# PSUM banks and ScalarE copies in a fused attention and SwiGLU kernel: three banks for attention, two for down-projection groups, the first term of p by ScalarE while groups run, and every third down weight split three beats sooner

## The chip, the cores and the metric

The kernel runs on one core of one Trainium2 chip. The core has a matrix engine (TensorE, PE in the profile; its weight loads are the row PEld), VectorE (DVE), ScalarE (ACT), GpSimd (POOL) and SyncE (SP), which only issues DMAs here. Each engine takes its own instructions in the order in which they stand in its program; waits between engines go by semaphores. Matmul results go to PSUM, which this kernel uses as eight banks of 128 x 512 float32. The metric is the device time of one execution in microseconds; a comparison uses the median of several.

## The reference

One layer's input x (2048 x 576) goes through two branches, mixed by a sigmoid gate. Branch A is attention with 32 heads of 18 in four segments of 512 rows, each segment softmaxed causally within itself and adding a linear memory of the segments before. Branch B is a SwiGLU feed-forward with 4608 hidden units.

```python
g = _sigmoid((x * gate_w).sum(-1, keepdims=True))
a = _A_ref(x, A_wq, A_wk, A_wv, A_wo, A_beta)
b = _B_ref(x, B_w_gate, B_w_up, B_w_down)
return g * a + (1 - g) * b
...
logits = jnp.einsum("bhqd,bhkd->bhqk", qs, ks) * scale + mask
p = _softmax(logits, axis=-1)
a_dot = jnp.einsum("bhqk,bhkd->bhqd", p, vs)
...
return (_silu(x @ w_gate) * (x @ w_up)) @ w_down
```

Everything is float32. The kernel keeps that precision by splitting operands into a high and a low part and adding the products high x high, high x low and low x high.

## The kernel before, in words

The program is one long stream, written out by hand (the schedule is manual, so instructions stand in the order in which Python emits them). It has three stages: projections, memory updates and the gate; the main loop, in which the feed-forward and the attention run interleaved; and the output projection.

**The main loop** goes over `seq`: two halves of the rows (1024 each), and within each half 36 blocks `f` of 128 hidden units. One block makes gate and up for 128 units and 1024 rows with seven products instead of eight (a Strassen-like scheme). Each product, `seven`, is six matmuls of L985 and one of L988. ScalarE and VectorE evict and combine the results in three banks of their own (a, x, y: banks 0, 1, 2), at L1042 to L1067, and the hidden units are then split into `hh` (high, on ScalarE) and `hl` (low, on VectorE).

After each product comes a `tick`, eight per block, counted k = 0 to 7. A tick first issues loads of the down weight (`draw`, 128 x 576) and its split, where the tables say so, then calls `beat`. A beat does three things, in this order:
1. It runs the functions that are due. `defer(k, fn)` puts a function k beats ahead. Weight preparation hangs on this: sums on GpSimd (L245), high parts on ScalarE (L249), low parts on VectorE (L252), and the residue rows of the weights (`r_block`), which are stored in three parts: the high part `rt` (L231) is stored twice (L228), then VectorE overwrites `rt` with the low part (L232), which is stored too. L232 has to wait until the first stores have read `rt`. `BLOCKS` says which blocks of the first half make residues: 3, 6, 9, ..., 30, two each in the first four of them.
2. It runs down-projection groups, as many as `SHARE[k]` says: 0, 0, 2, 2, 3, 3, 3, 3. A group (`down_group`) is nine matmuls (L844) for 128 rows and 320 or 256 output columns over three blocks f, and its sum is added to `ya` on VectorE (L849, the first time a copy, L847).
3. Between the groups it advances the attention generator by one step, as far as its credit reaches.

Every third block (f % 3 == 0, f > 0) starts by queueing 16 groups, and its eight beats work them all off; such a block is called a group block here. While groups are queued a beat is busy and gives attention one step per odd-numbered slot; in the two blocks between, it gives about three steps per block. At the change of halves, ten beats without products (`BREAK`) work off the last 16 groups of the first half, while the operands of the second half (`xo`) are split.

**One attention step** (`att_gen`, tau) handles three score tiles at different stages. `p_bank(tau - 3)` makes p's first term (L745, float32 to float16) and, on GpSimd, its second (L746: what the first leaves over). `e_bank(tau - 1)` makes the exponentials (L731, ScalarE) and masks the diagonal on GpSimd (L739). `s_bank(tau)` makes scores (L713, TensorE) and their row bound `mb` (L719, VectorE), which the exponentials need. `x_bank(tau - 5)` transposes p by DMA (`pt`, L750, issued by SyncE), and every sixth step `v_unit` multiplies five transposed tiles with the values (L761, L762) and VectorE reduces the result (L768). Score tiles and value tiles take turns on the banks of `ts_tile`. A matmul that starts a new tile in a bank has to wait until the engine that reads the old one is done: L731 for a score tile, L768 for a value tile, L849 for a down group. p and the exponentials have four buffers each, transposed p has seven.

**Down weights**: `d_load` at ticks (0, 3), (1, 3), (2, 2), given as (f % 3, k); `d_split` at ticks (1, 1), (1, 7), (2, 7) queues the high part on ScalarE for that beat (L927), the low part on VectorE for the next (L928) and, in the fifth, a store of both to DRAM (`dc`, L826), from where the second half fetches them.

Of the kernel before, what the change touches and what calls it, by code (L numbers as in the profile page):

```python
# [16 lines left out]
AF = mybir.ActivationFunctionType  # L17
# [3 lines left out]
P = 128  # L21
# [44 lines left out]
def gated_mix(ctx, tc, xT, xrest, wf, wfr, wfh, wd, wv, wo, beta, cmask, ident, bmask, out):  # L66
    nc = tc.nc
# [31 lines left out]
    def banks(*ids):  # L99
        turn = cycle(ids)  # L100
        return lambda shape=(P, L): ps.tile(list(shape), F32, name=f"bank{next(turn)}")
# [3 lines left out]
    pair_tile = banks(3, 4)  # L105
# [4 lines left out]
    a_tile = banks(0)  # L110
    x_tile = banks(1)
    y_tile = banks(2)
    ts_tile = banks(5, 6)
    group_tile = banks(3, 4, 7)

    def split(hi, lo, src):
        nc.scalar.activation(hi, src, AF.Copy)  # L117
# [87 lines left out]
    def d_load(f):  # L205
        r = fp.tile([P, D], F32, name="draw", bufs=1)
        nc.sync.dma_start(r, wd[f])
        return r
# [468 lines left out]
    with ExitStack() as st:  # L677
        cps = []
# [63 lines left out]
        def p_bank(z):  # L742
            pe = cur.pop(("e", z))
            p = cur["p", z] = ap.tile([P, 2, L], F16, name="p", bufs=4)
            nc.vector.tensor_copy(p[:, 0], pe)  # L745
            nc.gpsimd.tensor_sub(p[:, 1], pe, p[:, 0])  # L746

        def x_bank(z):
# [36 lines left out]
        def att_gen():  # L785
# [5 lines left out]
            for tau in range(N + 10):  # L791
                u, n = divmod(tau, 6)
                if n == 2 and sends:
                    nc.sync.dma_start(*sends.pop(0))
                if 1 <= n <= 3 and u + 1 < 2 * NB:
                    for d in stack_loads(u + 1)[3 * n - 3:3 * n]:
                        nc.sync.dma_start(*d)
                if n == 2 and u > 1 and u % 2 == 1 and (u - 3) // 2 < NB:
                    o_step((u - 3) // 2)
                z = at(tau - PL)  # L800
                if z is not None:
                    p_bank(z)
                z = at(tau - 1)
                if z is not None:
                    e_bank(z)
                z = at(tau)
                if z is not None:
                    s_bank(z)
                if n == 5 and 1 <= u <= 2 * NB:
                    v_unit(u - 1)  # L810
                    if u % 4 == 1 and u // 4 + 1 < 4 * NSEG:
                        v_fetch(u // 4 + 1)
                z = at(tau - XL)
                if z is not None:
                    x_bank(z)
                yield
# [6 lines left out]
        def d_split(f, r):  # L823
            d = d_tile()
            split_by(1, d[:, 0], d[:, 1], r)
            defer(5, lambda: nc.sync.dma_start(dc[f], f32(d).rearrange("p a n -> p (a n)")))  # L826
            return d

        def d_fetch(f):
            d = d_tile()  # L830
            nc.sync.dma_start(f32(d).rearrange("p a n -> p (a n)"), dc[f])
            return d

        def down_group(c, i, hf, hs, ws, ya, half):
            b, k = divmod(i, 4)
            cs = (slice(0, 320), slice(320, D))[hf]
            t = (pair_tile if cps else group_tile)([P, 320])[:, :cs.stop - cs.start]
            n = 0
            for f in range(CH * c, CH * c + CH):
                hh, hl = (z[:, b, P * k:P * k + P] for z in hs[half, f])  # L840
                d = ws[half, f]
                dh, dl = d[:, 0], d[:, 1]
                for p, q in ((hh, dh), (hh, dl), (hl, dh)):
                    nc.tensor.matmul(t, p, q[:, cs], start=(n == 0), stop=(n == 3 * CH - 1))  # L844
                    n += 1
            if c == 0:
                nc.vector.tensor_copy(ya[:, i, cs], t)  # L847
            else:
                nc.vector.tensor_add(ya[:, i, cs], t, ya[:, i, cs])  # L849
            if c == FT // CH - 1 and hf and half == 0:  # L850
                stores.append((ffd[i], ya[:, i]))
# [5 lines left out]
        def c_open():  # L857
            if cps:
                return
            ast.close()  # L860
            cps.append(pool(st, "cp", 2, side="right"))
            for hf in range(2):
                wos.append(cps[0].tile([P, 2, NT, 288], F32R, name=f"wo{hf}", bufs=1))
            for n, (hf, z) in zip((1, 2, 4, 5, 8, 9), ((0, 0), (0, 1), (0, 2), (1, 0), (1, 1), (1, 2))):
                wo_load(n, hf, slice(96 * z, 96 * z + 96))
            defer(2, lambda: tiles.update({0: c_load(0)}))
            defer(6, lambda: tiles.update({1: c_load(1)}))
# [53 lines left out]
        defer(6, lambda: v_fetch(0))  # L921
        groups = []
        credit = [-1.0]
        yas = {}

        def split_by(k, hi, lo, src):
# [3 lines left out]
        def beat(k=None, half=0):  # L930
            for fn in due.popleft() if due else ():
                fn()
            busy = 1 if groups else 0
            share = 2 if k is None else SHARE[k]
            for n in range(max(share, 1)):
                if groups and n < share:
                    down_group(*groups.pop(0))
                if n % 2 or (not busy and (n or k in QUIET)):
                    continue
                credit[0] += 0.5 if k is None else TICK[half][busy]  # L940
                if credit[0] >= 1:
                    credit[0] -= 1
                    if next(att, att) is att:
                        c_open()
# [48 lines left out]
        for pos, (half, f) in enumerate(seq):  # L993
            if f == 0:
                yas[half] = yp.tile([P, 8, D], F32, name="ya")
            q = f % CH
# [21 lines left out]
            def tick():  # L1018
                k = step[0]
                step[0] += 1  # L1020
                if k == 0:
                    while stores:
                        nc.sync.dma_start(*stores.pop(0))
                if half == 0:
                    if (q, k) in ((0, 3), (1, 3), (2, 2)):
                        draw[f] = d_load(f)
                    if (q, k) in ((1, 1), (1, 7), (2, 7)):
                        g = f - 1 if k == 1 else f
                        ds[half, g] = d_split(g, draw.pop(g))
                elif (q, k) in ((1, 0), (1, 2), (2, 1)):  # L1030
                    g = f - 1 if k == 0 else f
                    ds[half, g] = d_fetch(g)
                beat(k, half)
# [7 lines left out]
            seven(a, 0)  # L1041
            nc.scalar.activation(xx, a, AF.Copy)  # L1042
            tick()
            seven(y, 1)
            nc.scalar.activation(p5, y, AF.Copy)
# [29 lines left out]
            if f == FT - 1:  # L1075
                groups += feed(half, f)
                if half == 0:
                    for n in range(BREAK):
                        beat(None if n > 1 else n)
                    XO, XR = X2, XR2  # L1080
                    assert not groups
# [13 lines left out]
        def downs(k):  # L1095
            for _ in range(min(k, len(groups))):
                down_group(*groups.pop(0))

        ffs = {n: f_load(n) for n in range(2)}
        for n in range(17):  # L1100
# [6 lines left out]
            if n:  # L1107
                tt = order[n - 1]
                ff = ffs.pop(n - 1)
                for hf in range(2):  # L1110
                    c = slice(288 * hf, 288 * hf + 288)
                    t = chain_tile()
# [67 lines left out]
```

## Time and profile before

| | us |
|---|---|
| median of 3 runs (1762.95 to 1763.73) | 1763.63 |
| the profiled execution | 1765.94 |
| its span, first to last instruction | 1764.2 |
| TensorE busy in the span | 1720.6 |
| clock granted to TensorE, mean | 0.993 |

Rows are read like this. In the busy table and the windows, a number is busy time in us, with the count of instructions in brackets; a window's row ends with the granted clock, the mean share of DMA engines that were busy, and GB/s. In the waits, `PE bank L713 <- ACT pe L731: 13.2, 19, 1.2` says that the TensorE instruction of line 713 that writes a bank waited for the ScalarE instruction of line 731 that writes pe: 13.2 us in all, 19 times, 1.2 us the longest. A group of instructions has line, engine, operation, out<-in, shapes and count, then busy us and mean ns of one, then the idle time before them and who ended it. In the timeline a row starts with its start in us from the span's start and its duration in us; square brackets hold the idle time of that engine just before it and what ended it. Two instructions of an engine may overlap slightly. Buffer numbers are left out of names.

### The profile page before, as it was taken

The numbers are of one execution on the slowest core, as the hardware profiler recorded it, in microseconds if no ns is written. First come the engines' busy times: TensorE is split into PE (matmuls) and PEld (weight loads), VectorE is DVE, ScalarE is ACT, GpSimd is POOL, SyncE is SP. The second block draws the span as 40 slices with busy tenths as digits, with TensorE's granted clock in tenths as the row PEclk, the third lists the DMA queues.
The fourth block names the chain that finished last, engine by engine and source line by source line (L and its number), as shares of the span: only waits on it lengthen the run. The fifth ranks groups of instructions, "written<-read, shape, count | busy, mean of one in ns | idle before, by whom it ended". The sixth has DMA issues, their size and how long they took to land.

```text
span 1764.2 us, 34937 instructions
## 1 busy us (share of the span) xinstructions
PE 1720.6 (98%) x11868; PEld 1490.4 (84%) x11868; DVE 1366.7 (77%) x3239; ACT 1095.4 (62%) x2201; POOL 933.7 (53%) x1194
## 2 busy tenths in 40 slices
PE   9999999999999999999998999999999999999999
PEld 7898978788888888887887888888888888888899
DVE  6566578888898888888888677788788777887655
ACT  7665575775676577566656756665766576556511
POOL 4434545566565655655556455555555555555221
PEclk9999999999999999999999999999999999999999
DMA  8653489898998988898979976876777677756534
GB/s 283 222 188 117 164 287 192 209 223 178 220 221 197 186 190 205 174 203 186 202 163 250 280 163 137 187 169 160 160 175 169 150 165 180 169 129 150 166 129 141
DMA packets 524003, 328.06 MB, mean 186 GB/s; under 512 B 411184, under 2 KB 460336, under 8 KB 523824
## 3 DMA queue, kind: packets, MB, share of 16 engines
q1 hardware_dynamic: 523824, 325.83, 75.3%
q8 instruction: 93, 1.52, 0.4%
q14 instruction: 86, 0.70, 0.1%
HBM read 165.76 MB, written 76.09 MB: 137 GB/s over the span
## 4 chain that ended last, share of the span: by engine, by line
PE 76%; ACT 11%; DVE 4%; DMA 3%; issue 3%; POOL 2%; SPq 1%; DVEq 0%; ACTq 0%; POOLq 0%
PE bank L985 27%; PE bank L844 25%; PE bank L140 10%; PE bank L988 4%; PE bank L713 3%; PE bank L761 2%; ACT L1059 2%; ACT pe L731 1%; ACT L978 1%; PE bank L762 1%; PE bank L399 1%; ACT row L1059 1%; DMA pt<-p 1%; ACT bank L1042 1%; PE bank L445 1%
## 5 line engine op out<-in xcount | busy, mean ns | idle before, releaser
L746 POOL TENSOR_TENSOR p<-pe,p 128x512 f16<-128x512 f32 x320 | 374.3, 1170 | 474.7 <-DVE p L745 447.6
L844 PE MATMUL bank<-dw,hh 128*128 128x320 f32 (+1 forms) x2304 | 492.4, 306 | 3.0 <-ACT hh L117 2.9
L844 PEld LDWEIGHTS bank<-dw,hh 128*128 128x128 f32 x2304 | 384.4, 191 | 14.1 <-ACT hh L117 3.1
L731 ACT ACTIVATE pe<-bank,mb 128x512 f32<-128x512 f32 (+3 forms) x512 | 246.1, 522 | 227.3 <-DVE mb L719 224.5
L844 PE MATMUL bank<-dw,hl 128*128 128x320 f32 (+1 forms) x1152 | 342.1, 297 | 0.0
L719 DVE CUSTOM_DVE_ANT_0 scr<-bank,cm 128x512 bf16<-128x512 f32 (+3 forms) x512 | 246.1, 481 | 7.3 <-PE bank L713 0.6
L849 DVE TENSOR_TENSOR ya<-bank,ya 128x320 f32<-128x320 f32 x352 | 158.1, 453 | 82.8 <-PE bank L844 81.9
L844 PEld LDWEIGHTS bank<-dw,hl 128*128 128x128 f32 x1152 | 219.5, 191 | 0.2 <-DVE hl L118 0.2
L988 PE MATMUL bank<-xr,rh 128*128 128x512 f32 x504 | 196.6, 390 | 0.0
L739 POOL TENSOR_SCALAR_AFFINE_SELECT pe<-pe 128x256 f32<-128x256 f32 (+1 forms) x320 | 150.2, 470 | 31.4 <-ACT pe L731 25.9
L745 DVE CAST p<-pe 128x512 f16<-128x512 f32 x320 | 144.3, 451 | 1.4 <-DMA pt<-p 1.4
L713 PE MATMUL bank<-kst,qst 108*128 108x512 bf16 (+3 forms) x512 | 125.2, 306 | 13.3 <-ACT pe L731 13.2
L245 POOL TENSOR_TENSOR ws<-raw 128x256 f32<-128x256 f32 x140 | 120.9, 864 | 18.3 <-DVE wo__22862 L252 4.1
L988 PEld LDWEIGHTS bank<-xr,rh 128*128 128x128 f32 x504 | 94.7, 188 | 20.5
L928 DVE TENSOR_TENSOR hl<-row,hh 128x512 fp32r<-128x512 f32 x120 | 100.9, 841 | 10.7 <-ACT hh L927 10.3
L1052 ACT ACTIVATE row<-bank 128x512 f32<-128x512 f32 x72 | 43.1, 599 | 100.3 <-PE bank L988 100.2
L1057 DVE TENSOR_TENSOR row<-bank,row 128x512 f32<-128x512 f32 x72 | 49.6, 689 | 59.0 <-ACT bank L1056 58.8
L1059 ACT ACT_TABLE_LOAD x72 | 92.4, 1283 | 1.3
L978 ACT ACT_TABLE_LOAD x72 | 92.4, 1283 | 1.0
L761 PE MATMUL bank<-v,pt 128*128 128x57 bf16 x1280 | 77.6, 188 | 12.0 <-ACT pe L731 10.9
L713 PEld LDWEIGHTS <-qst 108*128 108x128 bf16 x512 | 35.8, 98 | 63.1 <-issue 47.0
L140 PE MATMUL bank<-xo,qhi 128*128 128x512 f32 x264 | 83.1, 396 | 0.0
(2165 smaller groups left out, 4114.0 us busy)
## 6 DMA issues: line engine op xcount, KB each, us to landing
raw<-in_wf_dram SPq DMA_DIRECT2D x140, 256.0 KB
rh<-rc SPq DMA_DIRECT2D x72, 336.0 KB
dc<-dw SPq DMA_DIRECT2D x36, 576.0 KB
dw<-dc SPq DMA_DIRECT2D x36, 576.0 KB
stk<-q SPq DMA_DIRECT2D x32, 384.0 KB
draw<-in_wd_dram SPq DMA_DIRECT2D x36, 288.0 KB
rc<-rt SPq DMA_DIRECT2D x42, 224.0 KB
vd<-vps SPq DMA_DIRECT2D x8, 912.0 KB
```

What stands on the lines that cost most here:

```text
L140: nc.tensor.matmul(t, st[n], mv[n], start=(n == 0), stop=(n == 13))
L713: nc.tensor.matmul(t[:, c:c + w], qs[:KR, pr, P * i:P * i + P], ks[:KR, pr, 0:w], start=True, stop=True)
L719: nc.vector.tensor_tensor_reduce(scr[:, :w], t[:, c:c + w], cm[:, L - w:L], -SCALE, 3.0e38, OP.add, OP.min, m[:, k:k + 1])
L731: nc.scalar.activation(pe[:, c:c + w], t[:, c:c + w], AF.Exp, bias=m[:, k:k + 1], scale=SCALE)
L739: nc.gpsimd.affine_select(d, d, pattern=pat, compare_op=OP.is_ge, fill=0.0, base=0, channel_multiplier=1)
L745: nc.vector.tensor_copy(p[:, 0], pe)
L746: nc.gpsimd.tensor_sub(p[:, 1], pe, p[:, 0])
L844: nc.tensor.matmul(t, p, q[:, cs], start=(n == 0), stop=(n == 3 * CH - 1))
L849: nc.vector.tensor_add(ya[:, i, cs], t, ya[:, i, cs])
L985: nc.tensor.matmul(t, w[:, p, z], x[z][:, q], start=first and n == 0, stop=False, skip_group_check=True)
L988: nc.tensor.matmul(t, rem[:, RPOS[j]], XR[j], start=False, stop=True, skip_group_check=True)
L1059: nc.scalar.activation(sg0, sg0, AF.Silu)
```

## The change

`ts_tile` takes turns on banks 5, 6, 7 instead of 5, 6. `group_tile` (banks 3, 4, 7) goes; down groups always use `pair_tile` (banks 3, 4). p's first term is a ScalarE activation (Copy) in beats that begin with groups queued, and stays on VectorE in the others. The third split of down weights is queued at tick (2, 4) instead of (2, 7).

```diff
-    ts_tile = banks(5, 6)
-    group_tile = banks(3, 4, 7)
+    ts_tile = banks(5, 6, 7)
...
             p = cur["p", z] = ap.tile([P, 2, L], F16, name="p", bufs=4)
-            nc.vector.tensor_copy(p[:, 0], pe)
+            if mode[0]:
+                nc.scalar.activation(p[:, 0], pe, AF.Copy)
+            else:
+                nc.vector.tensor_copy(p[:, 0], pe)
             nc.gpsimd.tensor_sub(p[:, 1], pe, p[:, 0])
...
-            t = (pair_tile if cps else group_tile)([P, 320])[:, :cs.stop - cs.start]
+            t = pair_tile([P, 320])[:, :cs.stop - cs.start]
...
         credit = [-1.0]
+        mode = [0]
...
-            busy = 1 if groups else 0
+            busy = mode[0] = 1 if groups else 0
...
-                    if (q, k) in ((1, 1), (1, 7), (2, 7)):
+                    if (q, k) in ((1, 1), (1, 7), (2, 4)):
```

In the built program the order on TensorE and GpSimd is the same as before but for bank names; 219 instructions go from VectorE to ScalarE; and twelve splits of down weights, with their stores in SyncE's queue, stand earlier.

## The prediction

> **What bounds the kernel now.** I read the page's totals, then the windows of the main loop on TensorE alone, then TensorE's waits.
>
> ```profile
> PE 1720.6 (98%) x11868; PEld 1490.4 (84%) x11868; DVE 1366.7 (77%) x3239; ACT 1095.4 (62%) x2201; POOL 933.7 (53%) x1194
> ...
> 300.00:940.00 640.00, 625.05 (x4493) 1.00 0.87 196
> 1000.00:1620.00 620.00, 614.18 (x4389) 1.00 0.73 164
> ...
> PE bank L713 <- ACT pe L731: 13.2, 19, 1.2
> PE bank L761 <- ACT pe L731: 10.9, 8, 4.1
> PE bank L761 <- DMA pt<-p: 1.0, 3, 0.5
> ```
>
> TensorE is busy for all but 43.6 us of 1764.2, so this change can only win idle time, not work. In 300 to 940 us it idles 14.95 us, in 1000 to 1620 us 5.82 us, and nearly all of that has one name: a score matmul (L713) or the first value matmul (L761) waits until the exponentials (L731) have read the bank that it wants to overwrite. That is 13.2 + 10.9 = 24.1 us in 27 waits. The same waits, asked for by stretch:
>
> ```profile
> PE bank L713 <- ACT pe L731: 9.6, 13, 1.2
> PE bank L761 <- ACT pe L731: 4.6, 5, 1.8
> ...
> PE bank L713 <- ACT pe L731: 3.6, 6, 0.9
> PE bank L761 <- ACT pe L731: 2.2, 2, 1.2
> ```
>
> The first pair is 260 to 945 us (14.2 us, 18 waits), the second 1000 to 1660 us (5.8 us, 8 waits); the remaining one, the longest of the whole run at 4.1 us, is at the change of halves. The exponentials are late because of VectorE, which hands out work strictly in order:
>
> ```profile
> POOL p L746 <- DVE p L745: 447.6, 277, 5.5
> ACT pe L731 <- DVE mb L719: 224.5, 127, 4.6
> ...
> L745 DVE CAST p<-pe 128x512 f16<-128x512 f32 x320 | 144.3, 451 | 1.4 <-DMA pt<-p 1.4
> L354 ACT ACTIVATE q<-qr 128x512 bf16<-128x512 f32 x36 | 22.5, 624 | 7.5 <-DVE qr L351 6.9
> L927 ACT ACTIVATE dw<-draw 128x576 fp32r<-128x576 f32 x36 | 24.2, 673 | 0.0
> L928 DVE TENSOR_TENSOR dw<-draw,dw 128x576 fp32r<-128x576 f32 x36 | 28.6, 796 | 4.5 <-ACT dw L927 4.5
> ```
>
> ScalarE idles 224.5 us waiting for the row minimum (L719), GpSimd 447.6 us for the first term of p (L745); both stand in VectorE's queue.
>
> **The third attention bank.** Score and value tiles take turns on three banks instead of two, so a tile waits for the reader of the tile three back. All 27 waits end on the tile two back; the tile three back was read at least 1.7 us, mostly 5 to 9 us, before the stalled matmul could have started (the readers' ends against the matmuls' starts, tile by tile). So all 24.1 us of this wait go; the question is what is late next. I split them.
> (a) Eleven of the 18 waits before 945 us fall on the first ticks of a block with down groups, 8.5 us in all, and all 8 after 1000 us, 5.8 us: ScalarE and VectorE recover there, since the groups give them time. I count 14.3 us as won.
> (b) Seven, from the first to the last row below, fall in the block just before, where every tick is a 1.6 us gate product and both helper engines are full: 5.7 us.
>
> ```profile
> 324.69 0.19 PE L761 MATMUL bank<-v,pt 128*128 128x57 bf16 x1 [1.00 <-ACT pe L731]
> 814.39 0.38 PE L713 MATMUL bank<-kst,qst 108*128 108x128 bf16 x2 [1.17 <-ACT pe L731]
> 816.61 0.70 DVE L1049 TENSOR_TENSOR bank<-bank,row 128x512 f32<-128x512 f32 x1
> 817.95 0.53 PE L985 MATMUL bank<-xo,wo__11068 128*128 128x512 f32 x1
> 940.49 0.38 PE L713 MATMUL bank<-kst,qst 108*128 108x128 bf16 x2 [1.15 <-ACT pe L731]
> ```
>
> At 814 us, with the 1.17 us gone, the product at 817.95 would come at 816.8, but it overwrites the bank that L1049 reads until 817.3: 0.5 us of 1.17 are lost again. I take half of 5.7: 2.9 us (from 0 to all of it).
>
> **p's first term on ScalarE.** While groups are queued, 219 of the 320 copies move (the instruction order of the changed kernel). VectorE loses 219 x 0.451 = 99 us. A ScalarE cast from SBUF to f16 is not in the trace; the bf16 one of the same shape takes 0.624 us, so ScalarE gets 137 us more and goes from 62% to 70%. It has cover: the 224.5 us of waiting for minima, which also shrink because two copies leave the queue ahead of them. Behind a copy on ScalarE stand the exponentials and the products' evictions, and behind those TensorE; without cover a copy costs up to 0.62 us there. The eviction that TensorE needs first in these blocks (L1042) is issued before the copy, so I take 0. The copy also takes over the wait for the transpose that still reads p's old buffer: 1.4 us over 320 so far, taken as 0 more, up to 1.7 us each where it is late (the rc<-rt wait below). Earlier p should shorten the 1.0 us for transposes; I take half, 0.5 us.
>
> **Two banks for down groups.** A group lasts about 1.2 to 1.6 us and its sum (L849) frees the bank; now it must be done when the group after next starts. In the trace it would be late 49 times. Two kinds:
>
> ```profile
> 460.68 0.42 DVE L745 CAST p<-pe 128x512 f16<-128x512 f32 x1
> 462.54 0.95 DVE L745 CAST p<-pe 128x512 f16<-128x512 f32 x1
> 465.65 0.48 DVE L849 TENSOR_TENSOR ya<-bank,ya 128x320 f32<-128x320 f32 x1
> ...
> 465.37 0.30 PE L844 MATMUL bank<-dw,hh 128*128 128x320 f32 x1
> ...
> 468.51 0.54 SPq L228 DMA_DIRECT2D rc<-rt  x1
> 472.85 0.62 DVE L232 TENSOR_TENSOR rt<-rr,rt 128x448 fp32r<-128x448 f32 x1 [1.68 <-DMA rc<-rt]
> 473.39 0.48 DVE L849 TENSOR_TENSOR ya<-bank,ya 128x320 f32<-128x320 f32 x1
> 472.23 0.31 PE L844 MATMUL bank<-dw,hh 128*128 128x320 f32 x1
> ```
>
> First group: its sum ends at 466.13, the third group starts at 465.37, 0.76 us late. But 0.42 + 0.95 us of copies ahead of it go, and so does the down weight's 0.8 us: no wait. Fifth group: VectorE stands 1.68 us before L232 for a store, and the sum ends at 473.87, 1.64 us after the seventh group's start at 472.23. No copy lies between, so this remains, shortened only by as much as GpSimd, which waits for copies less, makes rt's input earlier; I take 0.8 us in the early blocks that still make such residues and 0.2 us in the later ones. The worst lateness of each group block, summed, is 9.1 us; I take 4.5 us (from 1 to 9).
>
> **Every third weight split three beats sooner.** Twelve times 0.67 us on ScalarE and 0.80 us on VectorE leave the crowded first beats of a group block for the fifth and sixth beat before it: same sum. ScalarE could stand there for the load:
>
> ```profile
> 632.14 0.59 SPq L207 DMA_DIRECT2D draw<-in_wd_dram  x1
> 635.25 0.60 ACT L1056 ACTIVATE bank<-bank 128x512 f32<-128x512 f32 x1
> 464.31 0.42 SPq L826 DMA_DIRECT2D dc<-dw  x1
> ```
>
> The tightest case leaves 3.7 us from issue to the end of L1056, after which the split now stands; the other eleven leave more. The store rc<-rt above took 4.3 us from issue to release, so 0 to about 0.6 us; I take 0. Behind the split stand SiLU's table and SiLU, needed by nothing for 1 us. The store dc<-dw moves three beats up SyncE's queue, past loads and two transposes, at 0.42 us of issue each: off the path, 0 (up to 1 us if a transpose is pushed into a value tile).
>
> **The change of halves.**
>
> ```profile
> 951.92 0.21 PE L761 MATMUL bank<-v,pt 128*128 128x57 bf16 x1 [4.09 <-ACT pe L731]
> 957.66 0.31 PE L844 MATMUL bank<-dw,hh 128*128 128x320 f32 x1
> ...
> 953.78 0.84 ACT L731 ACTIVATE pe<-bank,mb 128x256 f32<-128x256 f32 x2 [1.39 <-DVE mb L719]
> 954.51 0.63 ACT L117 ACTIVATE xo<-wo__12969 128x512 fp32r<-128x512 f32 x1
> ...
> 955.17 1.30 DVE L118 TENSOR_TENSOR xo<-wo__12969,xo 128x512 fp32r<-128x512 f32 x1 [0.22 <-ACT xo L117]
> 956.39 1.65 DVE L928 TENSOR_TENSOR hl<-row,hh 128x512 fp32r<-128x512 f32 x1
> 957.96 0.81 DVE L849 TENSOR_TENSOR ya<-bank,ya 128x320 f32<-128x320 f32 x2
> ...
> 951.90:957.20 5.30, 5.28 (x55) 5.28 (x55) 5.04 (x10) 2.88 (x6) 4.24 (x4) 0.50 1.09 363
> ```
>
> The 4.09 us wait goes, and the first two groups run early. The third group then needs the first one's bank, and that sum stands behind two splits for the second half, which stand behind two exponentials on ScalarE. With two p copies ahead of them there, ScalarE ends the xo split about where it does now, the sum ends near 958.1 instead of 958.43, and the third group starts there instead of 957.66. TensorE also runs at 0.50 of its clock until 957.20 after its wait; a new wait of some 5 us would bring that back for the 3 to 5 us behind 958.1, half of which is about 2.2 us. So nothing of 4.1 us is won and 2.6 us are lost (from a win of 1 to a loss of 5).
> [...]
>
> **The sum.** Won 14.3 + 2.9 + 0.5 = 17.7 us; lost 4.5 + 2.6 = 7.1 us; net 10.6 us. The profiled execution took 1765.94 us (its span 1764.2), so it would take 1755.3; the median of the runs is 2.3 us lower, 1763.63 - 10.6 = 1753.0 us.
>
> **Rivals.**
> - All of it is won: copies leave VectorE and the sums are never late. 14.3 + 5.7 + 1.0, and at the change of halves 2: 23 us, 1741. For: ScalarE's and GpSimd's idle times; against: L232 waits for a store, not for a copy.
> - The next wait takes its place: (b) returns whole, half of (a) too as ScalarE, with 137 us more, is late with evictions, and sums cost 7: 17.7 - 2.9 - 7 - 7 - 2.6 leaves about -1.8, 1765: no change beyond noise. For: both helpers are full in the blocks between; against: ScalarE waits over 1 us before most exponentials.
> [...]
> [...]
>
> **How the numbers follow.** Forecast 62%, all won 13%, no change 13%, slower 12%. The forecast's own range is 5 to 17 us of gain, 1747 to 1759. For 8 in 10: the low end takes (b) whole, 1 us of late sums, and nothing at the change of halves, 20 us, 1743; the high end half of (b), half of (a) lost and 7 us of late sums, hardly a gain, 1763. What a measurement of this kernel can tell is 0.2%, 3.5 us: faster 62 + 13 + 5 of the no-change cases = 80%; same 9%; slower 11%.
>
> **What would show it.** L713 and L761 waiting for L731: near 0. A new row L844 waiting for L849: 3 to 8 us, its longest at the change of halves, near 955. L745 on ScalarE near 0.62 us, 219 of them; ScalarE's waits for minima well under 224 us, GpSimd's waits for p too. L985 waiting for L1049 or L1042: 2 to 4 us. Wrong if L844's waits exceed 15 us, if between 300 and 1620 us a clock of 0.50 shows anywhere but at the change of halves, or if evictions on ScalarE stall TensorE in group blocks.

## The result, and the profile after

The changed kernel takes 1767.69 us (median of 17 runs, 1765.04 to 1772.16) against 1763.35 us for the kernel before (17 runs, 1761.57 to 1765.73). The ratio is 1.0026, 95% interval 1.0019 to 1.0034: 0.26% or 4.3 us slower, where 10.6 us faster was forecast and 1743 to 1763 us was the range.

The profiled execution of the changed kernel took 1767.69 us, its span 1766.0 us. The profiled execution of before was 2.6 us above its own median, so this pair of profiles differs by less than the medians do. First the busy totals and three groups of instructions of the changed kernel, then TensorE's waits. Lines have moved: L844 is now L846 (down groups), L849 is L851 (their sums), L713 is L712, L761 is L763, L731 is L730, L719 is L718, L232 is L231, L252 is L251; p's first term is L745 on ScalarE and L747 on VectorE.

```profile
PE 1723.4 (98%) x11868; PEld 1485.0 (84%) x11868; DVE 1280.7 (73%) x3020; ACT 1208.3 (68%) x2420; POOL 932.3 (53%) x1194
...
L748 POOL TENSOR_TENSOR p<-pe,p 128x512 f16<-128x512 f32 x320 | 381.0, 1193 | 391.5 <-DVE p L747 182.8
L846 PE MATMUL bank<-dw,hh 128*128 128x320 f32 (+1 forms) x2304 | 495.8, 308 | 21.6 <-DVE ya L851 17.0
L846 PEld LDWEIGHTS bank<-dw,hh 128*128 128x128 f32 x2304 | 382.0, 190 | 40.9 <-DVE ya L851 25.7
...
L730 ACT ACTIVATE pe<-bank,mb 128x512 f32<-128x512 f32 (+3 forms) x512 | 246.6, 522 | 119.1 <-DVE mb L718 118.9
...
L745 ACT ACTIVATE p<-pe 128x512 f16<-128x512 f32 x219 | 135.8, 625 | 14.1 <-DMA pt<-p 8.3
```

```profile
PE bank L846 <- DVE ya L851: 17.0, 21, 3.0
...
PE bank L763 <- DMA pt<-p: 2.9, 2, 1.6
...
PE bank L846 <- DVE ya L849: 1.8, 2, 1.3
PE bank L988 <- DVE bank L1052: 1.6, 2, 1.1
```

The load moved, though by less than forecast: 86 us left VectorE (99 forecast), 113 us came to ScalarE (137 forecast). ScalarE's waits for minima shrank from 224.5 to 118.9 us. GpSimd's waits for p's first term were 447.6 us, all for VectorE; now they are 182.8 us for VectorE and, where the term comes from ScalarE, 156.5 us for ScalarE:

```profile
POOL p L748 <- DVE p L747: 182.8, 94, 5.3
POOL p L748 <- ACT p L745: 156.5, 60, 7.8
```

No score or value matmul waits for the exponentials any more: the 24.1 us have no row. In their place stand 18.8 us in which a down group waits for the sum that frees its bank, a wait that had no row before.

The windows of the main loop show where that happens: the first half gained nothing (625.05 us of TensorE in 640 before), the second half did (614.18 in 620 before). The clock is 1.00 in both.

```profile
300.00:940.00 640.00, 624.13 (x4473) 526.57 (x4472) 507.35 (x1189) 474.71 (x946) 382.19 (x508) 1.00 0.86 195
1000.00:1620.00 620.00, 618.30 (x4397) 528.97 (x4396) 454.68 (x1119) 452.01 (x904) 341.60 (x442) 1.00 0.76 167
```

To find the place more closely I took, in both traces, the time from the first product matmul of each block to that of the next (L985 before, L988 after), summed by kind of block. "First half" is the 11 group blocks f = 3 to 33, "second half" the 11 of f = 39 to 69, "between" the first half's other blocks, "change" the block f = 35 with the beats of `BREAK`. Differences to the profile of before, in us:

| kernel | first half | between | change | second half |
|---|---|---|---|---|
| changed kernel | +9.6 | -3.6 | +2.0 | -3.3 |
| e1 two banks for groups alone | +9.7 | -0.2 | +1.4 | +2.1 |
| e2 copies alone | +6.7 | -2.1 | +0.5 | +4.9 |
| e3 banks alone | +10.8 | -4.1 | +3.6 | -3.7 |
| e8 banks and copies | +11.4 | -4.5 | +3.1 | -3.3 |
| e6 changed, residue's low part on GpSimd | +0.9 | -5.6 | +2.7 | -3.3 |
| e10 e6 and a third bank at the change | -0.5 | -4.4 | -1.0 | -3.3 |
| e11 e6 and one low part later | -3.0 | -5.7 | +1.4 | -5.5 |
| e12 both | -3.2 | -4.5 | -0.9 | -5.5 |
| e13 before, copies from the third beat on | +1.2 | -0.3 | 0.0 | -0.3 |
| e14 e12, copies from the third beat on | +2.9 | -5.8 | +0.9 | -3.8 |

The other blocks of the second half differ by 0.1 us at most, the stages ahead of the loop and behind it by up to 2 us from one profile to the next, also where only one line of the first half is changed (e9, 2.0 us). In the column "between", 1.6 us of the figures of e2, e6, e11 and e14 lie in the very first block, ahead of all groups: in the profile of before, as in those of the other rows, the clock is at half for 3.4 us there (0.50 from 233.6 to 237.0 us), in these four it is not. These 1.6 us belong to the execution and not to an edit: e10 has e6's edit and not the difference.

Inside the group blocks I sorted the time from one matmul's start to the next one's by the two matmuls' kinds. In the changed kernel the steps into a score or value matmul shrank by 10.2 us in the first half and 7.1 us in the second: 17.3 us won. The steps into and within down groups grew by 19.5 and 3.7 us: 23.2 us lost. With -3.6 between, +2.0 at the change and 0.4 of other steps that is 4.7 us slower, beside 4.3 us between the medians.

The 23.2 us have few places. For each of the 16 groups of a block, this is the growth of the step into its first matmul, summed over the 11 blocks of a half (groups not listed: under 0.5 us in the changed kernel):

| kernel | third, first half | seventh, first half | sixteenth, first half | third, 13th and sixteenth, second half |
|---|---|---|---|---|
| changed kernel | 1.3 | 11.4 | 4.1 | 2.8 |
| e3 banks alone | 15.0 | 2.6 | 0.7 | 1.9 |
| e8 banks and copies | 7.4 | 6.9 | 4.2 | 2.8 |
| e6 | 1.5 | 0.0 | 4.3 | 2.8 |
| e12 | 2.1 | 0.0 | 0.5 | 0.9 |
| e14 | 7.6 | 0.0 | 0.6 | 2.2 |

The seventh group is late by 0.93 to 1.51 us in each of the ten blocks that make a residue, and by 0.00 in the eleventh (f = 33), which makes none. The timeline of the changed kernel at one of them (f = 24):

```profile
718.78 0.45 PE L846 MATMUL bank<-dw,hh 128*128 128x320 f32 x2
...
719.65 0.69 DVE L1060 TENSOR_TENSOR row<-bank,row 128x512 f32<-128x512 f32 x1 [1.86 <-ACT bank L1059]
...
720.24 1.17 POOL L748 TENSOR_TENSOR p<-pe,p 128x512 f16<-128x512 f32 x1 [3.04 <-ACT p L745]
720.26 1.62 DVE L231 TENSOR_TENSOR rt<-rr,rt 128x448 fp32r<-128x448 f32 x1
...
721.80 0.48 DVE L851 TENSOR_TENSOR ya<-bank,ya 128x320 f32<-128x320 f32 x1
...
722.33 0.30 PEld L846 LDWEIGHTS bank<-dw,hh 128*128 128x128 f32 x2 [0.98 <-DVE ya L851]
722.34 0.56 PE L846 MATMUL bank<-dw,hh 128*128 128x320 f32 x2 [0.78 <-DVE ya L851]
```

The same block in the kernel before, VectorE's rows:

```profile
716.37 0.63 DVE L232 TENSOR_TENSOR rt<-rr,rt 128x448 fp32r<-128x448 f32 x1 [0.31 <-DMA rc<-rt]
716.91 0.48 DVE L849 TENSOR_TENSOR ya<-bank,ya 128x320 f32<-128x320 f32 x1
```

Before, the residue's low part waits 0.31 us for the store and takes 0.63 us, with nothing on GpSimd beside it. After, it waits for nothing (no bracket) but takes 1.62 us: GpSimd's subtraction for p, which now comes earlier, starts 0.02 us ahead of it and runs beside it. Without that extra 1 us the 0.78 us for which the seventh group's first matmul waits would not be there. The mean over all 14 residues says the same; first VectorE's group before, then after:

```profile
L232 DVE TENSOR_TENSOR rt<-rr,rt 128x448 fp32r<-128x448 f32 x14 | 9.5, 681 | 6.6 <-DMA rc<-rt 3.8 <-DMA kst<-stk 2.5
```

```profile
L231 DVE TENSOR_TENSOR rt<-rr,rt 128x448 fp32r<-128x448 f32 x14 | 15.5, 1108 | 6.5 <-DMA rc<-rt 3.0 <-POOL pe L738 1.5 <-POOL p L748 1.1
```

The wait ahead of it is unchanged (6.6 and 6.5 us in all); its duration went from 681 to 1108 ns. At f = 24, with GpSimd beside it, 1.62 us took the place of 0.63, and this block is not alone. In nine of the fourteen residues of the changed kernel L231 starts while a subtraction of GpSimd is running, 0.02 to 0.70 us after that one's start, and takes 0.95 to 1.62 us. In all nine it ends 0.48 us after GpSimd's subtraction ends, however early or late it began.

The sixteenth group is late for a like reason, in the last beat of a block (f = 24 again, changed kernel): a weight's low part of 1.39 us stands ahead of the sum of the fourteenth group.

```profile
737.81 1.39 DVE L251 TENSOR_TENSOR wo__9610<-ws,wo__9610 128x256 fp32r<-128x256 f32 x1
...
739.13 0.41 DVE L851 TENSOR_TENSOR ya<-bank,ya 128x256 f32<-128x256 f32 x1
...
739.59 0.50 PE L846 MATMUL bank<-dw,hh 128*128 128x256 f32 x2 [0.48 <-DVE ya L851]
```

In the kernel before, the same low part takes 0.41 us, and GpSimd's next subtraction for p starts only later, at 733.57:

```profile
732.41 0.41 DVE L252 TENSOR_TENSOR wo__9610<-ws,wo__9610 128x256 fp32r<-128x256 f32 x1
```

At the change of halves the 4.09 us wait is gone, and a new one stands later (changed kernel, timeline and windows):

```profile
958.82 0.63 ACT L116 ACTIVATE xo<-wo__12969 128x512 fp32r<-128x512 f32 x1
...
959.48 1.46 DVE L117 TENSOR_TENSOR xo<-wo__12969,xo 128x512 fp32r<-128x512 f32 x1 [1.49 <-ACT xo L116]
...
960.87 0.88 DVE L931 TENSOR_TENSOR hl<-row,hh 128x512 fp32r<-128x512 f32 x1
961.68 0.81 DVE L851 TENSOR_TENSOR ya<-bank,ya 128x320 f32<-128x320 f32 x2
962.21 0.50 PEld L846 LDWEIGHTS bank<-dw,hh 128*128 128x128 f32 x2 [3.25 <-DVE ya L851]
```

```profile
953.40:956.70 3.30, 1.86 (x19) 1.39 (x17) 2.04 (x4) 3.27 (x7) 0.28 (x2) 0.99 0.97 330
956.70:966.90 10.20, 7.24 (x28) 6.66 (x29) 5.41 (x12) 6.25 (x12) 8.59 (x8) 0.50 1.07 365
966.90:968.00 1.10, 1.10 (x10) 1.10 (x9) 0.76 (x2) 0.00 (x0) 0.00 (x0) 1.00 1.21 285
```

The sum stands behind the `xo` split, which stands behind ScalarE's copies and exponentials. The granted clock is 0.50 from 956.7 to 966.9, 10.2 us (before: from 950.4 to 957.2, 6.8 us). It fell before the new wait began: TensorE waits from 959.25 to 962.21, and in the 3.3 us ahead of 956.7 it had stood 1.27 us for a transposed p and less than 0.2 us for a low part. So the new wait didn't bring the half clock about; whether it made it last longer isn't shown.

### The profile page after: what moved, and what is told of

The parts are those of the page before. It is cut to its first block, busy times and chain, and to the rows that moved or that the text cites. A ratio compares the mean times of both kernels' runs of the same rounds, so it can differ in the third digit from the quotient of the medians.

```text
span 1766.0 us, 34859 instructions
## 1 busy us (share of the span) xinstructions
PE 1723.4 (98%) x11868; PEld 1485.0 (84%) x11868; DVE 1280.7 (73%) x3020; ACT 1208.3 (68%) x2420; POOL 932.3 (53%) x1194
## 4 chain that ended last, share of the span: by engine, by line
PE 75%; ACT 7%; DVE 5%; DMA 5%; issue 4%; POOL 3%; SPq 1%; DVEq 0%; POOLq 0%; ACTq 0%
PE bank L988 31%; PE bank L846 21%; PE bank L139 10%; PE bank L991 5%; PE bank L712 3%; PE bank L763 2%; DMA rc<-rt 1%; PE bank L764 1%; ACT L1062 1%; POOL ws L244 1%; ACT L981 1%; PE bank L398 1%; DMA kst<-stk 1%; ACT pe L730 1%; PE bank L444 1%
## 5 line engine op out<-in xcount | busy, mean ns | idle before, releaser
L748 POOL TENSOR_TENSOR p<-pe,p 128x512 f16<-128x512 f32 x320 | 381.0, 1193 | 391.5 <-DVE p L747 182.8
L846 PE MATMUL bank<-dw,hh 128*128 128x320 f32 (+1 forms) x2304 | 495.8, 308 | 21.6 <-DVE ya L851 17.0
L846 PEld LDWEIGHTS bank<-dw,hh 128*128 128x128 f32 x2304 | 382.0, 190 | 40.9 <-DVE ya L851 25.7
L846 PE MATMUL bank<-dw,hl 128*128 128x320 f32 (+1 forms) x1152 | 341.7, 297 | 0.3 <-DVE hl L117 0.3
L730 ACT ACTIVATE pe<-bank,mb 128x512 f32<-128x512 f32 (+3 forms) x512 | 246.6, 522 | 119.1 <-DVE mb L718 118.9
L851 DVE TENSOR_TENSOR ya<-bank,ya 128x320 f32<-128x320 f32 x352 | 159.7, 454 | 131.3 <-PE bank L846 130.6
L718 DVE CUSTOM_DVE_ANT_0 scr<-bank,cm 128x512 bf16<-128x512 f32 (+3 forms) x512 | 246.1, 481 | 9.3 <-PE bank L712 2.3
L846 PEld LDWEIGHTS bank<-dw,hl 128*128 128x128 f32 x1152 | 219.1, 190 | 0.9 <-DVE hl L117 0.9
L745 ACT ACTIVATE p<-pe 128x512 f16<-128x512 f32 x219 | 135.8, 625 | 14.1 <-DMA pt<-p 8.3
L712 PE MATMUL bank<-kst,qst 108*128 108x512 bf16 (+3 forms) x512 | 125.8, 307 | 0.0
L1045 ACT ACTIVATE bank<-bank 128x512 f32<-128x512 f32 x72 | 41.6, 578 | 69.7 <-PE bank L991 69.7
L1059 ACT ACTIVATE bank<-bank 128x512 f32<-128x512 f32 x72 | 42.0, 583 | 62.2 <-PE bank L991 61.7
```

Of the source, the lines that this page charges most:

```text
L712: nc.tensor.matmul(t[:, c:c + w], qs[:KR, pr, P * i:P * i + P], ks[:KR, pr, 0:w], start=True, stop=True)
L718: nc.vector.tensor_tensor_reduce(scr[:, :w], t[:, c:c + w], cm[:, L - w:L], -SCALE, 3.0e38, OP.add, OP.min, m[:, k:k + 1])
L730: nc.scalar.activation(pe[:, c:c + w], t[:, c:c + w], AF.Exp, bias=m[:, k:k + 1], scale=SCALE)
L745: nc.scalar.activation(p[:, 0], pe, AF.Copy)
```

## The experiments

Each ratio is to runs of the kernel before that were made beside it, with its 95% interval.

### The parts, one at a time: e1, e2, e3, e4, e8

e1, the kernel before with two banks for groups:

```diff
-    group_tile = banks(3, 4, 7)
+    group_tile = banks(3, 4)
```

> Down groups on banks 3 and 4, attention still on two, bank 7 idle in the main loop; p stays on VectorE. Theory 1 (the sums of the down groups, late on two banks, eat the gain): no wait of attention is removed, so this shows their price bare: TensorE's waits for the sums (L849) of 12 to 25 us, and 10 to 25 us slower than before. Rival (the copies on ScalarE let GpSimd run beside VectorE and slow it, and only that makes the sums late): waits for the sums under 9 us and at most 6 us slower.

Measured: 1777.50 us, ratio 1.0075 [1.0063, 1.0087].

e2, the kernel before with the copies alone (the `mode` lines of the change, `ts_tile` and `group_tile` as before):

```diff
-            nc.vector.tensor_copy(p[:, 0], pe)
+            if mode[0]:
+                nc.scalar.activation(p[:, 0], pe, AF.Copy)
+            else:
+                nc.vector.tensor_copy(p[:, 0], pe)
...
+        mode = [0]
...
-            busy = 1 if groups else 0
+            busy = mode[0] = 1 if groups else 0
```

> Only p's first term moves to ScalarE in beats with groups; banks as before (two for attention, three for groups). Theory 1: VectorE is relieved, the exponentials come sooner, part of the 24.1 us of waits for them goes: 3 to 12 us faster. Rival: GpSimd beside VectorE slows VectorE's two-input instructions, evictions come late: 2 to 8 us slower.

Measured: 1776.35 us, ratio 1.0067 [1.0055, 1.0080].

e3, the banks alone:

```diff
-    ts_tile = banks(5, 6)
-    group_tile = banks(3, 4, 7)
+    ts_tile = banks(5, 6, 7)
...
-            t = (pair_tile if cps else group_tile)([P, 320])[:, :cs.stop - cs.start]
+            t = pair_tile([P, 320])[:, :cs.stop - cs.start]
```

> Only the banks move: three for attention, two for groups; p on VectorE, splits as before. Theory 1: the waits for exponentials go (24 us), the waits for the sums come and are longer than in the changed kernel, since p's copies stand before them: 5 to 15 us slower than before. Rival: sums are late by less than in the changed kernel: 5 to 15 us faster than before.

Measured: 1770.81 us, ratio 1.0040 [1.0027, 1.0053].

e4, copies and early split on the banks of before (the `mode` lines, and (2, 7) to (2, 4)):

> p's first term on ScalarE in beats with groups, and the third split three beats sooner; banks as before. Theory 1: the two parts that cost nothing, kept without the banks: 4 to 14 us faster than before, and faster than the copies alone by 0 to 3 us. Rival: 2 to 8 us slower than before.

Measured: 1776.80 us, ratio 1.0065 [1.0049, 1.0081].

e8, the changed kernel without the early split:

```diff
-                    if (q, k) in ((1, 1), (1, 7), (2, 4)):
+                    if (q, k) in ((1, 1), (1, 7), (2, 7)):
```

> The changed kernel without the earlier third split. If the earlier split relieves the start of group blocks: 1 to 5 us slower than the changed kernel, with more waiting of the third group for its bank. If it only moves work: within 1 us. If it crowds the block before: 2 to 5 us faster.

Measured: 1771.75 us, ratio 1.0033 [1.0021, 1.0045].

What follows. The third bank that the groups give up costs 13.8 us (e1), inside the 10 to 25 expected. The wait that was to show it did not come out: TensorE waits 5.6 us for the sums there, not 12 to 25, while the steps into and within down groups grew by 13.2 us in the group blocks. As a third bank for attention it wins only 6.7 of the 13.8 us back (e1 to e3), although no wait for exponentials is left. In group blocks the steps into score and value matmuls shrink by 17.3 us from e1 to e3, but TensorE then comes earlier to the groups and loses 12.3 us more there, most of it at the third group (5.0 us late in e1's first half, 15.0 in e3's). Copies and split on top of the banks change too little to tell, 1.0040 to 1.0033 to 1.0026 with overlapping intervals. But the place of the loss moves: the table of groups shows the third group 15.0 us late with the banks alone, 7.4 with the copies, 1.3 with the early split too, and the seventh 2.6, 6.9 and 11.4. What is taken out of VectorE's queue ahead of the third group's bank is waited for again at the seventh's and, from e3 to e8, at the sixteenth's. Part of the step from 6.9 to 11.4 is the store: VectorE stands 3.0 us ahead of L231 for it in the changed kernel, 0.3 in e8.

Without the third attention bank the copies cost 12.7 us (e2), and with the early split added the result is the same within the intervals (e4). Neither expectation named for these two runs held: 3 to 14 us faster, or 2 to 8 us slower. TensorE's waits for exponentials in e2 grow from 24.1 to 32.4 us:

```profile
PE bank L713 <- ACT pe L731: 19.2, 19, 1.4
PE bank L764 <- ACT pe L731: 13.2, 8, 4.6
```

and the timeline of e2 near the start of a group block (f = 24) shows the copy (L746 in this kernel) ahead of the exponentials for which TensorE stands:

```profile
702.57 0.61 ACT L746 ACTIVATE p<-pe 128x512 f16<-128x512 f32 x1
...
703.09 0.81 ACT L731 ACTIVATE pe<-bank,mb 128x256 f32<-128x256 f32 x2
...
703.96 0.38 PE L713 MATMUL bank<-kst,qst 108*128 108x512 bf16 x1 [1.35 <-ACT pe L731]
```

The waits grew by 8.3 us and the run by 12.7. In e2's profile three of them, of 1.88, 2.32 and 1.73 us, are each followed by 3.4 us at half clock, which makes some 5 us more (an estimate: half of three times 3.4 us):

```profile
828.90:832.30 3.40, 3.40 (x40) 2.94 (x37) 2.54 (x7) 3.15 (x8) 3.40 (x6) 0.51 0.59 90
893.80:897.20 3.40, 3.40 (x10) 2.72 (x10) 1.05 (x3) 2.06 (x5) 3.40 (x6) 0.50 0.71 91
1624.20:1627.60 3.40, 3.40 (x10) 2.73 (x10) 1.00 (x2) 2.06 (x5) 3.32 (x5) 0.51 0.99 103
```

In the profile of e4 the same three waits (1.96, 2.30 and 1.74 us) leave the clock at 1.00. That execution took 1770.48 us, 6.3 us less than the median of e4.

### The residue's low part: e6, e9, e5, e7

e6, the changed kernel with that instruction on GpSimd:

```diff
-                (o + 4, lambda: nc.vector.tensor_sub(t, a, f32(t))), (o + 5, lambda: keep(2))]
+                (o + 4, lambda: nc.gpsimd.tensor_sub(t, a, f32(t))), (o + 5, lambda: keep(2))]
```

> The changed kernel, with the residue's low part subtracted by GpSimd at the same beat instead of VectorE: nothing else moves. Theory 3: the seventh group's wait goes, 7 to 12 us faster than the changed kernel. Rival: the wait stays with the next instruction of VectorE's queue; at most 3 us faster.

Measured: 1758.29 us, ratio 0.9958 [0.9946, 0.9970].

e9, the same line in the kernel before:

> The kernel before, with the residue's low part on GpSimd: a control for the last run but one. If three group banks hid the late sum, as theory 3 has it, nothing is won: within 3 us of before. Rival (VectorE's relief is good by itself): 4 us or more faster than before.

Measured: 1765.71 us, ratio 1.0012 [1.0003, 1.0020].

What follows. Fourteen instructions moved off VectorE take the ratio from 1.0026 to 0.9958, some 12 us, and the seventh group's lateness goes from 11.4 to 0.0 us. The first half's group blocks get 8.7 us shorter; part of the rest may be the clock, which in e6's profile is at half for 3.4 us from 302.6 us and in the changed kernel's is not. In the kernel before the same move wins nothing, since a group there overwrites the bank of the group three back, whose sum is done. So this one instruction turned the change from a gain into a loss. On GpSimd it waits 24.6 us for the store, and nothing that the profile shows waits for it:

```profile
L231 POOL TENSOR_TENSOR rt<-rr,rt 128x448 fp32r<-128x448 f32 x14 | 16.2, 1154 | 25.5 <-DMA rc<-rt 24.6 <-issue 0.8
```

e5, the changed kernel with all residues made in the blocks after (no group runs there), and e7, the same in the kernel before:

```diff
-BLOCKS = {3: (4, 5), 6: (6, 7), 9: (8, 9), 12: (10, 11), 15: (12,), 18: (13,), 21: (14,), 24: (15,), 27: (16,), 30: (17,)}
+BLOCKS = {4: (4, 5), 7: (6, 7), 10: (8, 9), 13: (10, 11), 16: (12,), 19: (13,), 22: (14,), 25: (15,), 28: (16, 17)}
```

> The changed kernel, with the residue blocks moved from group blocks to the blocks after them (3, 6, ..., 27 to 4, 7, ..., 28, the last one to 28 too). Theory 3 (the seventh group waits because the residue's low part stands before its sum on VectorE, and GpSimd beside it makes it 1.6 us instead of 0.6): the 11.4 us that the seventh group's start lost in the first half's group blocks go, at most 4 us come back in the blocks between: 7 to 12 us faster than the changed kernel, 3 to 8 us faster than before. Rival (VectorE is full in group blocks, whatever stands where): at most 3 us faster than the changed kernel.

Measured: 1826.43 us, ratio 1.0345 [1.0331, 1.0359].

> The kernel before, with the same move of the residue blocks: a control. Three banks for groups hide a late sum, so theory 3 expects no gain: within 3 us of before, rather slower (the blocks between are full). Rival: the move is good by itself, 4 us or more faster than before.

Measured: 1821.24 us, ratio 1.0318 [1.0304, 1.0331].

What follows. Both are some 60 us slower, whichever banks are used, so they say nothing about banks; they show what VectorE standing still costs. None of the expected ranges held. In e7 the low part takes 625 ns, undisturbed, but VectorE stands 56.3 us ahead of it instead of 6.6, and the blocks between are 59.0 us longer:

```profile
L232 DVE TENSOR_TENSOR rt<-rr,rt 128x448 fp32r<-128x448 f32 x14 | 8.8, 625 | 56.3 <-DMA rc<-rt 39.3 <-ACT hh L927 14.1 <-DMA qst<-stk 3.0
```

The store ends later there; why was not followed. Part of the 59.0 us is the clock, which in e7 is at half in seven stretches of 3.4 or 6.8 us between 321 and 878 us, 34 us in all.

### What is left after that: e10, e11, e12

e10, e6 with three banks for the groups of the change of halves (bank 0 makes no products in those beats):

```diff
+    break_tile = banks(0, 3, 4)
+    brk = [0]
...
-            t = pair_tile([P, 320])[:, :cs.stop - cs.start]
+            t = (break_tile if brk[0] else pair_tile)([P, 320])[:, :cs.stop - cs.start]
...
+                    brk[0] = 1
                     for n in range(BREAK):
                         beat(None if n > 1 else n)
+                    brk[0] = 0
```

> The changed kernel with the residue's low part on GpSimd, and at the change of halves the down groups also take bank 0, which no product uses there. Theory 4 (the third group there waits for the first one's sum, which stands behind the second half's splits): the 4.0 us wait goes and the half clock behind it, 3 to 7 us faster than the same kernel without it (1758.3). Rival (the sums or the operands are late anyway): within 1.5 us.

Measured: 1754.01 us, ratio 0.9947 [0.9935, 0.9958]. The change of halves is 3.6 us shorter than in e6.

e11, e6 with the low part of the third weight made one beat later in group blocks, out of their last beat:

```diff
-            todo += [(HIGH[j], lambda j=j: high(j)), (LOW[j], lambda j=j: low(j))]
+            todo += [(HIGH[j], lambda j=j: high(j)), (LOW[j] + (j == 2 and f % CH == 1), lambda j=j: low(j))]
```

> The changed kernel with the residue's low part on GpSimd, and, in group blocks alone, the low part of the third weight operand one beat later, out of the last beat (three groups) into the next block's first. Theory 5 (the sixteenth group waits since that low part, slowed by GpSimd, stands before the fourteenth's sum): 4.3 us of the first half and about 1.9 us of the second go, 3 to 6 us faster than 1758.3. Rival (the operand is late for its product two products on): slower.

Measured: 1751.31 us, ratio 0.9931 [0.9919, 0.9943]. The sixteenth group's lateness goes from 4.3 to 0.6 us, the group blocks win 3.9 us in the first half and 2.2 in the second.

e12, both:

> Both of the two edits before. If they are apart in time, as theories 4 and 5 have it, their gains add: 6 to 12 us faster than 1758.3, about 1749. Rival: less than the sum by 3 us or more.

Measured: 1750.89 us (5 runs, 1748.81 to 1751.98), ratio 0.9925 [0.9913, 0.9937]: 13.1 us faster than the kernel before. TensorE's waits in it:

```profile
PE bank L765 <- DMA pt<-p: 5.6, 4, 1.6
PE bank L848 <- DVE ya L853: 4.9, 5, 2.5
```

What follows. By the ratios (e6 was run beside other runs of the kernel before) the third bank at the change is worth 0.0011, 1.9 us, with overlapping intervals, the later low part 0.0027, 4.8 us, and both 0.0033, 5.8 us. By the medians the two gains are 4.3 and 7.0 us and both together 7.4, 3.9 less than their sum, as the rival had it; by the ratios they fall short of their sum by 0.9 us. e12 can't be told from e11 by its time. Its change of halves is 2.3 us shorter; its blocks between are 1.2 us longer, but only through the clock in the very first block, as said below the first table. Whether the bank at the change is worth the 3.6 us of its stage or less stays open.

### What a copy on ScalarE costs: e13, e14

e13, the kernel before with the copies of e2, but only from the third beat of a block on (178 copies of 219; the first two beats hand out no group and keep VectorE), shown against e2:

```diff
-            busy = mode[0] = 1 if groups else 0
+            busy = 1 if groups else 0
...
+            mode[0] = busy and share > 0
```

> The kernel before, with p's first term on ScalarE only in beats that hand out groups (from the third beat of a block on); in the first two beats of a block with groups it stays on VectorE. If copies on ScalarE cost time because those at the start of such a block stand ahead of the exponentials for which the score and value matmuls wait there, this run lies within 4 us of the kernel before (1760 to 1768 us), and TensorE's waits for the exponentials come back from 32.4 to about 24 us. If it is the load of ScalarE as such, most of the 219 copies are still there, and the run stays 8 to 13 us above the kernel before.

Measured: 1764.93 us, ratio 1.0002 [0.9994, 1.0011]. TensorE's waits in it:

```profile
PE bank L713 <- ACT pe L731: 14.9, 20, 1.5
PE bank L764 <- ACT pe L731: 4.7, 6, 1.4
PE bank L764 <- DMA wo__13021<-in_xT_dram: 4.1, 1, 4.1
...
PE bank L764 <- DMA raw<-in_wf_dram: 1.8, 1, 1.8
```

e14, the same edit in e12:

> The version with the residue's low part on GpSimd, the third bank at the change of halves and the low parts of weights one beat later, with p's first term on ScalarE only from the third beat of a block on. If three attention banks take up the lateness of the exponentials anyway, the copies of the first two beats cost nothing there and moving them back to VectorE only loads VectorE where the first sums are late: 1751 to 1756 us. If ScalarE's copies ahead of the exponentials still cost time with three banks, it is faster: 1746 to 1749 us.

Measured: 1757.87 us, ratio 0.9968 [0.9955, 0.9980].

What follows. The 41 copies of the first two beats cost all of e2's 12.7 us; the other 178 cost nothing that can be measured, so it is their place in ScalarE's queue and not its load. The waits are back at 14.9 + 4.7 + 4.1 + 1.8 = 25.5 us, near the 24 expected. The last two rows name a DMA, but they are the waits of 4.1 us at the change of halves and of 1.8 us at 889 us that the profile of before puts down to the exponentials. With three attention banks it is the other way round: keeping the 41 copies on VectorE costs 0.0043, 7.6 us (e12 to e14), more than the 5 us at most that were expected, and the third group's lateness goes from 2.1 to 7.6 us, since VectorE is what the third group waits for.

## Why the prediction was wrong

**The third attention bank: right.** All 24.1 us of waiting for the exponentials went. In group blocks 17.3 us were won where 14.3 were forecast, in the blocks between 3.6 where 2.9 were. Products wait 1.6 us for L1052 and 0.7 for L1045 (L1049 and L1042 before): 2.3 us, within the 2 to 4 us expected. The 0.5 us for transposes did not come: they cost 2.9 us instead of 1.0. What the prediction's sum has no term for is that TensorE, coming earlier, then waits longer for the groups' sums (e1 to e3).

**p's first term on ScalarE: 0 by luck, and for this kernel only.** 625 ns each and 219 of them, as costed, and on top of the banks no loss that can be measured. But the 0 is what is left of two effects: from e3 to e8 the copies take 7.6 us of lateness from the third group and put 4.3 us on the seventh, 3.5 on the sixteenth and 0.9 on the groups of the second half. The prediction had the first effect, in the term for the groups, and not the second. The cover named for it, ScalarE's waits for minima, was the wrong one: alone, the same copies cost 12.7 us (e2). With the third attention bank the exponentials may be late: no wait for them is left in the changed kernel.

**The early split: right at 0** by the intervals of e8 and the changed kernel, and by luck too: it took 6.1 us of lateness from the third group and put 4.5 on the seventh, which the prediction did not have.

**The change of halves: right in size and place, not in the clock.** 2.0 us lost, 2.6 forecast, and the third group does stand behind the two splits. Counted from the first product of that block it starts after 23.3 us (23.5 before, 23.9 by the forecast's 958.1), so the loss is not in its start but in the 10.2 us at half clock. No run shows the forecast's 2.2 us for a half clock that a new wait of some 5 us brings: the 10.2 us began 2.5 us ahead of the wait, which was 2.96 us long. A third bank there (e10) shortens this stage by 3.6 us.

**Two banks for down groups: the step that failed.** The sum had 4.5 us for late sums, 9 at most; they cost 23.2 us, 19.8 of them at the first matmul of a group. TensorE's waits for the sums are 18.8 us, above the 15 us that the prediction gave as a sign of being wrong. The first group's sum behaves as argued (1.3 us at the third group). "Fifth group: ... this remains, shortened only ..., I take 0.8 us in the early blocks ... and 0.2 us in the later ones" is the failed sentence: the seventh group lost 0.93 to 1.51 us in every residue block, 11.4 in all. I had taken the store's wait for the cost and held L232's own duration, 0.62 us in the quoted row, for fixed. The wait did shrink where GpSimd came earlier (0.31 us to none at f = 24), but by the same step GpSimd's subtraction came to lie beside L232 and stretched it to as much as 1.62 us. The prediction used the first effect and missed the second. e6 shows that this instruction on VectorE is what the seventh group waits for. That its stretch comes from GpSimd is read from the traces (nine ends, each 0.48 us behind GpSimd's), and no run tested it by itself. The sixteenth group (4.1 + 1.9 us) was not foreseen at all, and could not be from the lateness in the trace of before: the fourteenth group's sum ends 0.12 us at most after the sixteenth's start there, and with the banks alone (e3) the sixteenth loses 0.7 us in the first half. It is the same missed effect: the copies bring GpSimd beside the low part ahead of that sum (0.41 us before, 1.39 us after at f = 24).

**The rivals.** Slower, at 12%, is what came, by 4.3 us. Its largest part is the fifth group's sum through L232: ten waits of about 1 us were enough, without any clock effect. The clock stayed at 1.00 with waits up to 1.6 us in the long windows. The rival of no change (1765 us) came within 3 us of the measured time by luck: it had the attention waits come back and 7 us for late sums, and neither is so.

With the late sums at 23.2 instead of 4.5 us the forecast's own sum turns from 10.6 us won to 8.1 lost; the attention waits won 3.7 us more than forecast, which leaves 4.4, about what was measured.

## What to carry to other kernels

When a bank is taken from a user, list for every tile in it the instructions that stand ahead of its reader in that reader's queue, all of them and not only the latest, and ask of each how long it takes if the schedule beside it shifts. A work item that moves to another engine changes more than two busy sums: its consumer runs earlier, and what runs beside the consumer can get slower (L231 took up to 1.62 us beside GpSimd here, 0.62 alone). Its place in the new engine's queue can matter more than its length: 41 copies ahead of exponentials cost 12.7 us here, 178 others nothing. After such a change the first thing to try is a move of the one instruction that stands ahead of the late reader: fourteen instructions of 0.6 us were worth some 12 us here, and nothing in the kernel whose groups had a third bank.

## What the runs showed of the hardware

**The low parts that VectorE subtracts took about twice as long beside GpSimd's instructions.** Counted over the weights' low parts (L252 before, L251 after, 128 x 256, 490 per run) by how much of each lies under a two-operand instruction of GpSimd: under 5% covered 417 ns both before and after, over 60% covered 881 and 893 ns. The residue's low part (L231) took 0.62 us alone and up to 1.62 us beside GpSimd. Each of the nine residues that start while GpSimd subtracts ended 0.48 us behind GpSimd's end.

**TensorE's idle time understated what a late bank cost.** In the changed kernel the matmuls of L846 show 17.0 us of waiting for L851 (3.0 of them at the change of halves), their weight loads 25.7 us, and the start-to-start growth of the groups is 23.2 us without the change of halves. In e1 it is 5.6 us of waiting against 13.2 us of growth. At the stall of 0.78 us ahead of 722.34 the weight load started late as well (0.98 us of waiting), and the first pair of matmuls took 0.56 us, against 0.45 at 718.78.

**The length of one wait did not tell whether the clock fell.** In e2 it went to 0.50 or 0.51 for 3.4 us after waits of 1.88, 2.32 and 1.73 us. In e4 it stayed at 1.00 after 1.96, 2.30 and 1.74 us in the same places, and in the kernel before after 1.80 us. In the changed kernel it fell at 956.7 us with no longer wait than 1.27 us in the 3.3 us ahead. So in these runs the length of one wait, up to 2.32 us, did not decide it.
